# By-pair attention for block 0 alone, key and value loads on 128 partitions, three blocks that share half the features, and an order planned twice

## The chip, the cores and the metric

The kernel runs on one core of a Trainium2 chip. The metric is device time in microseconds (us) of one execution. Three runs of the kernel before stand at 640.6, 641.05 and 642.23 us; the median, 641.05 us, is what the change is compared with. Five engines work side by side: PE (TensorE, matmuls), DVE (VectorE), ACT (ScalarE), POOL (GpSimd) and SP, which here only issues transfers. Each takes its instructions strictly in the order in which the program lists them.

## The reference

Three stages, one after the other, on 2304 tokens of 512 features (4 batches of 576 tokens, 8 heads of 64):

```python
kv = einsum('bhsd,bhse->bhde', k, v)                 # one 64x64 matrix per batch and head
out = einsum('bhsd,bhde->bhse', q, kv)
x = out / sqrt(mean(out**2, -1) + 1e-6) * g_norm     # tokens x 512
h = x @ w_in                                         # 512 -> 2048
y = (h * tanh(softplus(h))) @ w_out                  # 2048 -> 512
h2 = y @ w2_in                                       # 512 -> 1024
z = h2 * softmax(h2)
out = layernorm(z) * g_ln @ w2_out                   # 1024 -> 512
```

The weights come as 8-byte floats. Every matmul of the two expert stages is done as three fp16 matmuls (high times high, high times low, low times high; `PASS`).

## The kernel before, in words

Tokens are cut into 6 blocks of 384 (`BLK`). The hidden features of the first expert stage are cut into 4 groups of 512; a *unit* (b, g) is one block with one group. `H` of a unit is 4 matmul groups of 12 (`h_mm`, L557), `Y` of a unit again 4 groups of 12 (`y_mm`, L597). The second stage works on 18 token tiles: `2` (`emit_H2`, L674) is 24 matmuls, `O` (`emit_O`, L757) is 24 matmuls, and between them stands a softmax and layer norm on DVE and ACT and a transposing DMA (`s_T`, tile lnT).

**Weights** arrive in 48 pieces of 512 KB (`PIECES`): first features 0 to 1023 of w_in (8 pieces) and of w_out (8), then the second halves, then the second stage's. Each piece is decoded from 8 bytes to a high and a low fp16 half: ACT L505, POOL L510, DVE L515 and L522, ACT L533 (high), DVE L540 or L542 (low). There are 5 staging buffers, so the load of a piece waits for an earlier piece's L522.

**Attention** has two forms. *By pair* (functions `e_*`) works on transposed tiles of two heads in fp32, all on PE: transposes of q (L288), kv (L246), q times kv (L304), the sums of squares as a matmul with ones (L317), and the spread of the result over partitions as another (L337). *By tile* (functions `a_*`) works on 128 tokens with fp16 halves: q is split on ACT and DVE, transposed by DMA (L386, tile qT), multiplied on PE (L398), squared, summed and scaled on ACT, DVE and POOL, split into halves, and transposed by DMA again (L446, tile xT). The result of either, xT of a block, is what `H` of that block reads. Before the change blocks 0 and 1 go by pair and blocks 2 to 5 by tile.

kv of a batch is made in four pairs of heads (`kv_pair`): the 576 tokens lie as 96 partitions x 6 rows, and each pair is 12 matmuls of 64 columns, each of two recorded passes.

**The order** is made by a planner (`Plan.order`): each task has an engine, a cost in us, tasks that it follows, and sometimes a due time. The planner walks through the time, and gives a free engine the ready task with the earliest due time. The due times are worked back from `nominal`, a table of times that the list `pe` of PE's units gives. The table walks units two blocks at a time over the first half of the features: H of (0,0), (0,1), (1,0), (1,1), then the second half of blocks 0 and 1, and from block 2 on all four groups of a block. Y of the halves is kept as a partial sum (`y_part`, `y_sum`) for blocks 0 and 1.

What the planner puts out is five fixed lists. All plain loads but that of q of block 0 stand on SP's list, those of the weights among them, as do the transposing DMAs.

Of the kernel before, what the change touches and what calls it, by code (L numbers as in the profile page):

```python
# [7 lines left out]
FP32 = mybir.dt.float32  # L8
# [24 lines left out]
class Plan:  # L33
    def __init__(self):
        self.tasks = {}

# [3 lines left out]

    def order(self):
        tasks = self.tasks
        index = {k: n for n, k in enumerate(tasks)}
        followers = {k: [] for k in tasks}
        for k, t in tasks.items():
            for a in t[3]:
                followers[a].append(k)

        seen, topo = set(), []

        def visit(k):
            stack = [(k, iter(tasks[k][3]))]
            seen.add(k)
            while stack:
                at, it = stack[-1]
                for a in it:
                    if a not in seen:
                        seen.add(a)
                        stack.append((a, iter(tasks[a][3])))
                        break  # L60
                else:
                    topo.append(at)
                    stack.pop()

        for k in tasks:
            if k not in seen:
                visit(k)
        due = {}
        for k in reversed(topo):
            d = 1e9 if tasks[k][5] is None else tasks[k][5]  # L70
            for f in followers[k]:
                d = min(d, due[f] - tasks[k][1] - tasks[k][4])
            due[k] = d
        waits = {k: len(t[3]) for k, t in tasks.items()}
# [8 lines left out]
        while True:  # L83
            best = None
            for e, ks in open_.items():
                if ks:
                    at = max(free[e], min(ready[k] for k in ks))
                    if best is None or at < best[0]:
                        best = (at, e)
            if best is None:  # L90
                break
            at, e = best
# [5 lines left out]
            for f in followers[k]:  # L98
                waits[f] -= 1
                ready[f] = max(ready[f], end + tasks[k][4])  # L100
                if not waits[f]:
                    open_[tasks[f][0]].append(f)
        assert len(out) == len(tasks), [k for k in tasks if waits[k] > 0][:20]
# [4 lines left out]
def tile_attn_moe_moe2(  # L108
# [19 lines left out]
    R = 3  # L128
# [6 lines left out]
    KP = 96  # L135
    KR = S // KP
    PASS = ((0, 0), (0, 1), (1, 0))
    NST, NDEC, NG, NM = 5, 5, 3, 3

# [45 lines left out]
    yorder = [(0, 0), (0, 1), (1, 0), (1, 1), (0, 2), (0, 3), (1, 2), (1, 3)]  # L185
    yorder += [(b, g) for b in range(2, NB) for g in range(4)]
    line = ["H", "H", "H", "Y", "H", "Y", "Y"]
    while line.count("H") < NU:
        line += ["H", "Y"]
    hs, ys = iter(units), iter(yorder)  # L190
# [11 lines left out]

    raw = {}

    def load_pair(b, i):
        t = yT[(0 if b == 1 else 2) + i].rearrange("p c a t -> p (c a t)").bitcast(FP32)[0:KP]
        raw[b, i] = t.rearrange("p (a h r d) -> p a h r d", a=2, h=2, r=KR)
        for a, src in enumerate((k, v)):
            nc.sync.dma_start(
                out=raw[b, i][:, a],  # L210
                in_=src[b, 2 * i:2 * i + 2].rearrange("h (p r) d -> p h r d", r=KR),
# [4 lines left out]
    def load_q(b):  # L216
# [3 lines left out]
        while done < BLK:  # L220
            bb, s = divmod(t0 + done, S)
            n = min(BLK - done, S - s)
            (nc.scalar if b == 0 else nc.sync).dma_start(
# [7 lines left out]

    kvp_t = {}
    kvf = {}

    def kv_pair(b, i):
# [18 lines left out]
    HALF = [slice(0, 64), slice(64, 128)]  # L254

    def kv_full(b, i):

        c = slice(i, i + 1) if b == 0 else slice(0, 4)
        nc.scalar.activation(
            out=kvf[b][HALF[0], c, HALF[0]], in_=kvp_t[b][HALF[0]], func=ACTF.Copy)  # L260
        nc.vector.tensor_copy(out=kvf[b][HALF[1], c, HALF[1]], in_=kvp_t[b][HALF[1]])

    def kv_zero():
        nc.gpsimd.memset(kvr[0], 0.0)

    def kv_hi(b):
        for o in HALF:
            nc.scalar.activation(
                out=kvr[b % 2][o, 0, :, o], in_=kvp_t[b][o], func=ACTF.Copy, scale=32.0)

    def kv_lo(b):
        p = kvp_t[b]
        for o in HALF:
            nc.vector.scalar_tensor_tensor(
                out=kvr[b % 2][o, 1, :, o], in0=p[o], scalar=32.0,
                in1=kvr[b % 2][o, 0, :, o], op0=ALU.mult, op1=ALU.subtract,
# [22 lines left out]
    def e_xo(b, c):  # L299
        qT = eq_t.pop((b, c)).rearrange("p (r t) -> p r t", r=R)  # L300
        p = ex_t[b, c] = psY.tile([128, BLK], FP32, tag=f"y{c % 3}", name="xoT")
        p = p.rearrange("p (r t) -> p r t", r=R)
        for lo, hi, bb in ((0, 128, 0),) if b == 0 else ((0, 64, 0), (64, 128, 1)):
            nc.tensor.matmul(  # L304
                out=p[:, :, lo:hi], lhsT=kvf[bb][:, c], rhs=qT[:, :, lo:hi], start=True, stop=True)
# [6 lines left out]
    def e_ms(b, c):  # L312
        p, tag = (psH, "h") if b == 0 else ((psA, "a"), (psY, "y3"))[c % 2]
        er_t[b, c] = p.tile([128, 512], FP32, tag=tag, name="rT")
# [75 lines left out]
    def a_xo(b, r):  # L390
        qT = qT_t.pop((b, r))
        p = psA.tile([128, H, D], FP32, tag="a", name="xo")
# [693 lines left out]
```

## Time and profile before

| what | value |
|---|---|
| median of 3 runs | 641.05 us |
| profiled execution, its own time | 646.7 us |
| span in its profile | 644.9 us |
| PE busy | 624.8 us (97%) |
| DVE busy | 307.7 us (48%) |
| ACT busy | 269.2 us (42%) |
| POOL busy | 93.1 us (14%) |
| read from memory | 39.33 MB |
| mean granted TensorE clock | 0.986 of full speed |

The span runs from the first to the last instruction. "Busy" of PE counts a matmul from its start to its modelled end, so it is not a share of peak. In the chain of waits each row is a piece of the work that ended last: start, length, what. A row of a group of instructions gives the count, the busy time and the mean of one, and the idle time of the engine just ahead of them with what ended it.

### The profile page before, as it was taken

What the parts mean: (1) busy time and instruction counts of PE and PEld (TensorE: products, weight loads), DVE (VectorE), ACT (ScalarE), POOL (GpSimd) and SP (SyncE); (2) the same over time, 40 slices, a digit from 0 to 9 for tenths busy, and PEclk for the clock granted to TensorE, in tenths of its full rate; (3) what the DMA queues carried; (4) which work ended last, traced back from release to release, by engine and by line L of the source; (5) the groups of instructions that cost most, each with busy time, mean ns of one, the idle gap of its engine ahead of it and who ended that gap; (6) DMA issues with size and microseconds to landing.
All of it is one profiled execution on the core that took longest, in us unless ns stands there. A gap on an engine that the chain in (4) does not pass through costs nothing.

```text
span 644.9 us, 9802 instructions
## 1 busy us (share of the span) xinstructions
PE 624.8 (97%) x4010; PEld 355.0 (55%) x4010; DVE 307.7 (48%) x529; ACT 269.2 (42%) x461; POOL 93.1 (14%) x125
## 2 busy tenths in 40 slices
PE   7899998999999999999999999999999999999995
PEld 5557564666666666666666656665444444444441
DVE  0667887921633144212321239952835555455540
ACT  2568756541523243422332247642523433433340
POOL 1516422100200022001200122500000000000000
PEclk9989798999999999999999999999999999999998
DMA  9985497365340025002200055500342232324322
GB/s 258 270 223 180 134 290 216 80 134 145 66 82 1 1 50 79 4 0 42 41 2 2 17 180 171 188 1 1 66 99 49 66 82 66 83 65 99 77 71 65
DMA packets 92605, 60.41 MB, mean 94 GB/s; under 512 B 65680, under 2 KB 86160, under 8 KB 92560
## 3 DMA queue, kind: packets, MB, share of 16 engines
q1 hardware_dynamic: 91360, 59.00, 36.6%
q10 hardware_dynamic: 1200, 0.79, 0.4%
q8 instruction: 31, 0.51, 0.3%
q14 instruction: 14, 0.11, 0.1%
HBM read 39.33 MB, written 4.72 MB: 68 GB/s over the span
## 4 chain that ended last, share of the span: by engine, by line
PE 89%; DMA 6%; DVE 2%; ACT 2%; issue 1%; POOL 1%; SPq 0%; DVEq 0%; ACTq 0%; POOLq 0%
PE hp L557 27%; PE y L597 26%; PE op L757 15%; PE h L674 14%; DMA st<-in_moe_w_in_dram 2%; PE kvp L246 2%; DMA st<-in_moe_w_out_dram 1%; PE qTp L288 1%; PE xo L398 1%; DMA yT<-in_v_dram 1%; DMA xT<-xhl 1%; PE xoT L304 1%; PE rT L337 1%; DMA lnT<-hl 1%; PE rT L317 1%
## 5 line engine op out<-in xcount | busy, mean ns | idle before, releaser
L597 PE MATMUL y<-g,w 128*128 128x384 f16 x1152 | 204.7, 330 | 2.5 <-ACT yT L610 2.5
L557 PE MATMUL hp<-xT,w 128*128 128x384 f16 x1152 | 201.3, 327 | 3.0 <-ACT w L533 1.9
L597 PEld LDWEIGHTS <-w 128*128 128x128 f16 x1152 | 112.6, 99 | 78.8 <-issue 6.5
L557 PEld LDWEIGHTS <-w 128*128 128x128 f16 x1152 | 111.7, 98 | 78.6 <-ACT w L533 2.2
L567 ACT ACTIVATE m<-hp 128x384 f32<-128x384 f32 x96 | 46.9, 488 | 132.5 <-PE hp L557 131.9
L757 PE MATMUL op<-w,lnT 128*128 128x512 f16 x432 | 97.7, 384 | 4.2 <-DMA lnT<-hl 4.2
L579 DVE SCALAR_TENSOR_TENSOR g<-m,g 128x768 f16<-128x768 f32 x48 | 46.7, 973 | 110.6 <-ACT g L574 110.5
L674 PE MATMUL h<-w,yT 128*128 128x512 f16 x432 | 96.2, 379 | 0.0
L757 PEld LDWEIGHTS <-lnT 128*128 128x128 f16 x432 | 42.6, 99 | 56.5 <-DMA lnT<-hl 4.7
L674 PEld LDWEIGHTS <-yT 128*128 128x128 f16 x432 | 42.3, 98 | 50.4
L510 POOL TENSOR_SCALAR st<-st 128x512 f32<-128x512 f32 x48 | 42.7, 895 | 91.7 <-ACT P L505 71.3
L515 DVE SCALAR_TENSOR_TENSOR st<-st 128x512 int32<-128x512 int32 x48 | 37.1, 787 | 16.8 <-POOL st L510 16.8
L574 ACT ACTIVATE g<-m 128x768 f16<-128x768 f32 x48 | 40.4, 841 | 1.8 <-PE y L597 0.8
L691 ACT ACTIVATE e<-h,nb 128x1024 f32<-128x1024 f32 x18 | 20.1, 1114 | 48.9 <-DVE nb L686 44.4
L505 ACT ACTIVATE P<-st 128x512 f32<-128x512 f32 x48 | 31.9, 673 | 14.2 <-DMA st<-in_moe_w_out_dram 7.8
L522 DVE SCALAR_TENSOR_TENSOR P<-P,st 128x512 int32<-128x512 int32 x48 | 35.6, 759 | 0.2
L418 POOL TENSOR_SCALAR ms<-ms 128x8 f32<-128x8 f32 x12 | 2.6, 216 | 228.2 <-DVE ms L413 228.2
L698 DVE SCALAR_TENSOR_TENSOR z<-h,e 128x1024 f32<-128x1024 f32 x18 | 22.0, 1225 | 21.4 <-ACT e L691 21.4
L724 POOL TENSOR_SCALAR var<-var 128x1 f32<-128x1 f32 x18 | 3.4, 190 | 192.6 <-DVE var L719 192.6
L738 ACT ACTIVATE hl<-z 128x1024 f16<-128x1024 f32 x18 | 19.0, 1056 | 28.9 <-DVE z L733 28.9
L705 ACT ACTIVATE e<-z,nmz 128x1024 f32<-128x1024 f32 x18 | 20.7, 1147 | 23.7 <-DVE nmz L701 23.7
L742 DVE TENSOR_TENSOR hl<-z,hl 128x1024 f16<-128x1024 f32 x18 | 22.0, 1224 | 15.7 <-ACT hl L738 15.7
(96 smaller groups left out, 421.6 us busy)
## 6 DMA issues: line engine op xcount, KB each, us to landing
st<-in_moe_w_in_dram SPq DMA_DIRECT2D x24, 512.0 KB, 6.7
st<-in_moe_w_out_dram SPq DMA_DIRECT2D x24, 512.0 KB, 4.3
yT<-in_k_dram SPq DMA_DIRECT2D x16, 288.0 KB, 7.9
yT<-in_v_dram SPq DMA_DIRECT2D x16, 288.0 KB, 8.1
out_dram<-osb SPq DMA_DIRECT2D x18, 256.0 KB, 2.0
qraw<-in_q_dram SPq DMA_DIRECT2D x3, 768.0 KB, 6.3
qraw<-in_q_dram SPq DMA_DIRECT2D x4, 384.0 KB, 8.6
qraw<-in_q_dram ACTq DMA_DIRECT2D x1, 768.0 KB, 6.9
```

Of the source, the lines that this page charges most:

```text
L505: nc.scalar.activation(out=P, in_=v[:, :, 1], func=ACTF.Copy, scale=2.0 ** -111)
L510: nc.gpsimd.tensor_scalar(out=v[:, :, 1], in0=v[:, :, 1], scalar1=0.0, scalar2=1.0, op0=ALU.mult, op1=ALU.mult)
L515: nc.vector.scalar_tensor_tensor(out=v[:, :, 0], in0=v[:, :, 0], scalar=29, in1=v[:, :, 1], op0=ALU.logical_shift_right, op1=ALU.bitwise_or)
L522: nc.vector.scalar_tensor_tensor(out=P.bitcast(I32), in0=P.bitcast(I32), scalar=3, in1=v[:, :, 0], op0=ALU.logical_shift_left, op1=ALU.bit ...
L557: nc.tensor.matmul(out=h_t[b, grp, i], lhsT=w1[:, c, wa, f:f + 128], rhs=xT_t[b][:, C * xa + c], start=(c == 0 and m == 0), stop=(c == C - ...
L567: nc.scalar.activation(out=m_t[b, grp, i // 2][:, i % 2], in_=h_t.pop((b, grp, i)), func=ACTF.Mish, scale=2.0 ** -16)
L574: nc.scalar.activation(out=g_t[b, grp][:, 0, 2 * i:2 * i + 2], in_=m_t[b, grp, i], func=ACTF.Copy, scale=64.0)
L579: nc.vector.scalar_tensor_tensor(out=g_t[b, grp][:, 1, j], in0=m_t.pop((b, grp, i)), scalar=64.0, in1=g_t[b, grp][:, 0, j], op0=ALU.mult, ...
L597: nc.tensor.matmul(out=y_t[cc][:, 0:BLK], lhsT=w2[:, grp * G + ii, wa, cc * 128:(cc + 1) * 128], rhs=g_t[b, grp][:, ga, ii], start=(first ...
L674: nc.tensor.matmul(out=hp[:, half], lhsT=y[:, c, ya, tok], rhs=w3[:, c, wa, half * 512:(half + 1) * 512], start=(m == 0), stop=(m == 3 * C ...
L698: nc.vector.scalar_tensor_tensor(out=z, in0=T[t, "hp"], scalar=2.0 ** -14, in1=T[t, "e"], op0=ALU.mult, op1=ALU.mult, accum_out=sz)
L757: nc.tensor.matmul(out=op, lhsT=lnT[:, K2 * la + kk], rhs=w4[:, kk, wa], start=(m == 0), stop=(m == 3 * K2 - 1),)
```

## The change

1. Only block 0 goes by pair. Block 1 goes by tile like the others, with its three products in PSUM banks y0 to y2, which Y uses later. kv of batch 0 is kept in fp32 (`kvf[0]`) and its fp16 halves are made from that copy.
2. k and v of two heads lie on 128 partitions (head, then 64 parts of 9 tokens), so a pair is 18 matmuls of 64 rows and 64 columns in place of 12 of 96 rows.
3. Blocks 0, 1 and 2 (`NI`) go through the first half of the features before any goes through the second; block 2 gets a partial sum too, and xT of block 2 lies in the buffer of yT of block 5.
4. The planner plans twice: the times of the first plan become the due times of the second. Some costs are changed, the first loads stand in a line written by hand, and q of block 0 is loaded from SP.

```diff
-    KP = 96
-    KR = S // KP
+    KR = 2 * S // 128
+    NI = 3
...
-    units = [(0, 0), (0, 1), (1, 0), (1, 1), (0, 2), (1, 2), (0, 3), (1, 3)]
-    units += [(b, g) for b in range(2, NB) for g in range(4)]
+    units = [(b, 2 * half + g) for half in range(2) for b in range(NI) for g in range(2)]
+    units += [(b, g) for b in range(NI, NB) for g in range(4)]
...
     for r in range(KR):
             for h in range(2):
                 nc.tensor.matmul(
                     out=p[64 * h:64 * h + 64, j],
-                    lhsT=t[:, 0, h, r],
-                    rhs=t[:, 1, h, r],
+                    lhsT=t[HALF[h], 0, r],
+                    rhs=t[HALF[h], 1, r],
...
-        p = psA.tile([128, H, D], FP32, tag="a", name="xo")
+        p, tag = (psY, f"y{r}") if b == 1 else (psA, "a")
+        p = p.tile([128, H, D], FP32, tag=tag, name="xo")
...
     def y_ends(b, grp):
-        first = grp == 0 or (b < 2 and grp == 2)
-        last = grp == 3 or (b < 2 and grp == 1)
+        first = grp == 0 or (b < NI and grp == 2)
+        last = grp == 3 or (b < NI and grp == 1)
...
-    LAND = 1.9
+    LAND, PAIR, QLD, PIECE = 2.0, 2.15, 3.0, 1.6
...
-    tiles = [(b, r) for b in range(2, NB) for r in range(R)]
+    tiles = [(b, r) for b in range(1, NB) for r in range(R)]
...
+    w, kv = (lambda f: ("ld", ("1", f))), (lambda b, i: ("ld", b, i))
+    plan.line([
+        ("ldq", 0), kv(0, 0), kv(0, 1), w(0), kv(0, 2), kv(0, 3), w(1), w(2), w(3),
+        ("ldq", 1), kv(1, 0), kv(1, 1), w(4), kv(1, 2), w(5), kv(1, 3), w(6), w(7),
+    ])
...
+    for at_time, key in plan.order():
+        if plan.tasks[key][5] is not None:
+            plan.tasks[key][5] = at_time
     order = plan.order()
```

Where the instructions stand now is shown at three places.

PE, from the first kv pair on, before (kvp is a pair's kv, qTp a transposed q, xoT q times kv, rT the sums and the spread):

```order
L246 MATMUL kvp<-yT_104 64x64 x12
L288 MATMUL qTp<-ident,qraw 64x128 x24
L246 MATMUL kvp<-yT_105 64x64 x12
L304 MATMUL xoT<-qT,kvr_91 128x384 x2
L317 MATMUL rT<-ones,sq 128x2 x3
L246 MATMUL kvp<-yT_106 64x64 x12
```

and in the change, up to the first matmul of H (hp):

```order
L269 MATMUL qTp<-ident,qraw 64x128 x18
L233 MATMUL kvp<-yT_104 64x64 x18
L269 MATMUL qTp<-ident,qraw 64x128 x6
L233 MATMUL kvp<-yT_105 64x64 x18
L283 MATMUL xoT<-qT,kvf 128x384 x2
L294 MATMUL rT<-ones,sq 128x2 x6
L233 MATMUL kvp<-yT_106 64x64 x18
L314 MATMUL rT<-ident,rho 64x128 x6
L283 MATMUL xoT<-qT,kvf 128x384
L233 MATMUL kvp<-yT_107 64x64 x18
```

Three q transposes now stand ahead of the first kv pair, and a pair has 18 matmuls where it had 12.

SP, from the loads of batch 1's last kv pairs on, before (st is a weight piece, yT the buffer that k and v lie in, qraw is q):

```order
L460 DMA st<-in_moe_w_in_dram 128x4x256 x2
L209 DMA yT_105<-in_k_dram 96x2x384
L209 DMA yT_105<-in_v_dram 96x2x384
L468 DMA st<-in_moe_w_out_dram 128x1024 x5
L223 DMA qraw<-in_q_dram 128x8x192
L468 DMA st<-in_moe_w_out_dram 128x1024 x3
L460 DMA st<-in_moe_w_in_dram 128x4x256 x5
```

and in the change:

```order
L195 DMA yT_105<-in_v_dram 128x576
L441 DMA st<-in_moe_w_in_dram 128x4x256
L363 DMA_TRANSPOSE qT<-qhl 128x8x128
L441 DMA st<-in_moe_w_in_dram 128x4x256
L363 DMA_TRANSPOSE qT<-qhl 128x8x128 x2
L449 DMA st<-in_moe_w_out_dram 128x1024 x2
L209 DMA qraw<-in_q_dram 128x8x192
L449 DMA st<-in_moe_w_out_dram 128x1024 x2
L427 DMA_TRANSPOSE xT<-xhl 128x8x128
L449 DMA st<-in_moe_w_out_dram 128x1024 x2
L427 DMA_TRANSPOSE xT<-xhl 128x8x128
L363 DMA_TRANSPOSE qT<-qhl 128x8x128
```

The transposes of blocks 1 and 2 now stand between the loads of the weights, where before no transpose came until all of w_out was loaded.

ACT at the end of the program, before (e is the softmax, hl the split of the layer norm, osb the copy of a finished `O`):

```order
L765 ACTIVATE osb<-op 128x512
L738 ACTIVATE hl<-z 128x1024
L691 ACTIVATE e,S__5745<-h_5674,nb 128x1024
L705 ACTIVATE e,sq<-z,nmz 128x1024
L738 ACTIVATE hl<-z 128x1024
L765 ACTIVATE osb<-op 128x512 x2
```

and in the change:

```order
L746 ACTIVATE osb<-op 128x512
L719 ACTIVATE hl<-z 128x1024
L672 ACTIVATE e,S__5738<-h_5660,nb 128x1024
L686 ACTIVATE e,sq<-z,nmz 128x1024
L746 ACTIVATE osb<-op 128x512 x6
```

Behind the last tile's softmax stand six copies of an `O` in place of two: on PE seven `O` of 24 matmuls follow the last `2`, where before three did.

## Rows read from the trace of the kernel before

**Rows 1.** The page, section 2: 40 slices of the span, busy tenths of DVE, granted PE clock

```profile
DVE  0667887921633144212321239952835555455540
PEclk9989798999999999999999999999999999999998
```

**Rows 2.** The chain of waits, 0 to 75 us: start, length, what (pieces left out)

```profile
0.72 0.40 SPq L209
...
63.45 1.87 POOL rho L329
...
66.91 3.95 PE y L597 x12
70.87 4.23 PE hp L557 x25
```

**Rows 3.** PE's matmuls of H, 27.5 to 70.8 us: count, busy us, mean ns, idle

```profile
L557 PE MATMUL hp<-xT,w 128*128 128x384 f16 x97 | 19.0, 337 | 2.9 <-ACT w L533 1.9 <-DVE w L542 1.0
```

**Rows 4.** The chain of waits, 95 to 125 us, round the only later stop of PE

```profile
96.78 8.62 DMA st<-in_moe_w_out_dram
...
108.66 3.76 PE y L597 x12
112.41 1.95 PE hp L557 x12
```

**Rows 5.** The chain of waits, 600 to 645 us

```profile
614.60 5.18 PE h L674 x24
619.78 10.23 PE op L757 x48
630.01 4.29 DMA lnT<-hl
...
634.35 7.00 PE op L757 x24
```

**Rows 6.** Groups of PE's instructions by pair for block 0, 5 to 27.5 us

```profile
L288 PE MATMUL qTp<-ident,qraw 128*64 128x128 f32 x48 | 4.9, 393 | 0.0
...
L337 PE MATMUL rT<-ident,rho 128*64 128x128 f32 x48 | 3.5, 279 | 0.2 <-POOL rho L329 0.2
L304 PE MATMUL xoT<-qT,kvr 128*128 128x384 f32 x8 | 3.3, 519 | 0.0
L317 PE MATMUL rT<-ones,sq 128*128 128x2 f32 x24 | 3.3, 254 | 0.0
```

**Rows 7.** Groups of PE's instructions, 70.8 to 437 us

```profile
L597 PE MATMUL y<-g,w 128*128 128x384 f16 x1069 | 188.6, 328 | 2.5 <-ACT yT L610 2.5
...
L398 PE MATMUL xo<-kvr,qT 128*128 128x128 f16 (+1 forms) x180 | 10.1, 220 | 0.0
L246 PE MATMUL kvp<-yT 96*64 96x64 f32 x192 | 7.3, 226 | 0.0
```

**Rows 8.** DVE's groups, 27.5 to 70.8 us: decode of a piece of w_in, low half of kv

```profile
L515 DVE SCALAR_TENSOR_TENSOR st<-st 128x512 int32<-128x512 int32 x11 | 8.0, 729 | 5.4 <-POOL st L510 5.4
L522 DVE SCALAR_TENSOR_TENSOR P<-P,st 128x512 int32<-128x512 int32 x11 | 7.9, 724 | 0.1
L542 DVE SCALAR_TENSOR_TENSOR w<-P,gs,w 128x512 f16<-128x512 f32 x8 | 5.9, 745 | 2.0 <-ACT w L533 2.0
...
L274 DVE SCALAR_TENSOR_TENSOR kvr<-kvp,kvr 64x256 f16<-64x256 f32 x2 | 0.8, 422 | 0.0
```

**Rows 9.** DVE's groups over the whole span: low half of g, a step of attention by tile

```profile
L579 DVE SCALAR_TENSOR_TENSOR g<-m,g 128x768 f16<-128x768 f32 x48 | 46.7, 973 | 110.6 <-ACT g L574 110.5
...
L439 DVE TENSOR_TENSOR xhl<-xf,xhl 128x512 f16<-128x512 f32 x12 | 8.3, 690 | 5.3 <-ACT xhl L434 5.3
```

**Rows 10.** ACT's group, 27.5 to 70.8 us: high half of kv

```profile
L268 ACT ACTIVATE kvr<-kvp 64x256 f16<-64x256 f32 x2 | 0.8, 378 | 0.5 <-DVE kvf L261 0.5
```

**Rows 11.** Transfers issued at 131 to 140 us: KB, median us from issue to landing

```profile
qraw<-in_q_dram SPq DMA_DIRECT2D x1, 768.0 KB, 5.1
```

**Rows 12.** Transfers of the whole span

```profile
xT<-xhl SPq DMA_TRANSPOSE x12, 3.1
```

More of the change, by code (lines that the diff above doesn't have):

```diff
@@ L39, in add, with line @@
         self.tasks[key] = [engine, cost, fn, [a for a in after if a is not None], lag, due]
+    def line(self, keys):
+        for a, b in zip(keys, keys[1:]):
+            self.behind.setdefault(b, []).append(a)
     def order(self):
@@ L43, in order @@
         index = {k: n for n, k in enumerate(tasks)}
+        edges = {k: [(a, tasks[a][4]) for a in t[3]] + [(a, 0.0) for a in self.behind.get(k, ())]
+                 for k, t in tasks.items()}
         followers = {k: [] for k in tasks}
[L45 to L67, printed above, removed]
+        for k, es in edges.items():
+            for a, lag in es:
+                followers[a].append((k, lag))
+        waits = {k: len(es) for k, es in edges.items()}
+        topo = [k for k in tasks if not waits[k]]
+        for k in topo:
+            for f, _ in followers[k]:
+                waits[f] -= 1
+                if not waits[f]:
+                    topo.append(f)
+        assert len(topo) == len(tasks), [k for k in tasks if waits[k] > 0][:20]
         due = {}
         for k in reversed(topo):
[L70 to L74, printed above, removed]
+            due[k] = 1e9 if tasks[k][5] is None else tasks[k][5]
+            for f, lag in followers[k]:
+                due[k] = min(due[k], due[f] - tasks[k][1] - lag)
+        waits = {k: len(es) for k, es in edges.items()}
         ready = {k: 0.0 for k in tasks}
@@ L299, in e_xo @@
     def e_xo(b, c):
-        qT = eq_t.pop((b, c)).rearrange("p (r t) -> p r t", r=R)
+        qT = eq_t.pop((b, c))
         p = ex_t[b, c] = psY.tile([128, BLK], FP32, tag=f"y{c % 3}", name="xoT")
[L302 to L305, printed above, removed]
+        nc.tensor.matmul(out=p, lhsT=kvf[0][:, c], rhs=qT, start=True, stop=True)
     def e_sq(b, c):
@@ L827, in tile_attn_moe_moe2 @@
             if b == 3:
-                free = [("kv", 2, i), ("put", ("2", 15))]
-            task(("ld", b, i), "S", 1.8, load_pair, (b, i), free, LAND)
-    ring("qhl", 3, ("xo", 1, 3))
+                free = [("kv", 3, i - 2) if i > 1 else ("kv", 2, i + 2), ("put", ("2", 15))]
+            task(("ld", b, i), "S", PAIR, load_pair, (b, i), free, LAND)
+    for b in range(B):
+        for i in range(4):
+            task(("kv", b, i), "P", 0.92, kv_pair, (b, i),
+                 [("ld", b, i), ("kv", b, i - 1) if i else None], 0.25)
@@ L881, in tile_attn_moe_moe2 @@
-    kv_after = {2: [("kvz",)], 3: [("xo", 2, r) for r in range(R)]}
-    order_a = [2] + [(2, r) for r in range(R)] + [3] + [u for u in tiles if u[0] > 2]
+    task(("ldq", 0), "S", QLD, load_q, (0,), (), LAND)
+    for c in range(4):
+        u = (0, c)
+        bank = f"y{c % 3}"
+        task(("qT", *u), "P", 0.95, e_qT, u,
+             [("ldq", 0), ("ident",)] + ring(bank, 1, ("qc", *u)), 0.25)
+        task(("qc", *u), "A", 0.49, e_qc, u, [("qT", *u)] + (
+            ring("qT", 3, ("xo", *u)) if c < 3 else ring("xhl", 2, ("xo", *u))))
@@ L890, in tile_attn_moe_moe2 @@
+    for b in range(B):
+        every = [("kvf", 0, i) for i in range(4)] + [("zero",)] if b == 0 else [
+            ("kv", b, i) for i in range(4)]
+        if b:
+            plan.tasks["kv", b, 0][3] += bank_a[b]
+        if b > 1:
+            every += [("xo", b - 1, r) for r in range(R)]
+        task(("kvh", b), "A", 0.75, kv_hi, (b,), every)
         task(("kvl", b), "V", 0.8, kv_lo, (b,), [("kvh", b)])
@@ L923, in tile_attn_moe_moe2 @@
             else:
-                x = [("xlo", b, c) for c in range(C)] if b < 2 else [
+                x = [("xlo", b, c) for c in range(C)] if b == 0 else [
                     ("xT", b, r) for r in range(R)]
@@ L943, in tile_attn_moe_moe2 @@
     last_of, prev_y = {}, None
-    for n, (b, grp) in enumerate(yorder):
+    for n, (b, grp) in enumerate(units):
         T0 = nominal["Y", b, grp]
@@ L983, in tile_attn_moe_moe2 @@
          [("glo", *u, i) for u in units for i in range(2)]
[L984 removed]
+         + [("ylo", b, c) for b in range(NI) for c in range(C)] + [("open",)], 0.0)
     for t in range(NT2):
```

170 lines of the change are left out of this document (63 added, 107 removed).

## The prediction

> **What bounds the kernel now.** I read the page first. PE is busy over nearly the whole span, DVE in its first sixth and hardly later, and the granted TensorE clock dips once, in the slices round 70 us [rows 1]. So the time is PE's work and the places where PE does not do it, and those are to be looked for early and at the very end. The chain of waits says where. Up to 70.87 us it jumps between engines: PE waits for POOL's rho at 63.45, and only at 70.87 does H of block 1 begin [rows 2]. By then 96 matmuls of H (the row counts the next group's first too) and one group of Y are done [rows 3, 2], that is 8 + 1 of the 192 groups of 12; a group takes 1.95 at the full clock [rows 4]. From there the chain is PE alone, with one stop: ACT's queue stands behind a weight piece that landed late, PE sits idle for 2.5 [rows 7], and its next group takes 3.76 [rows 4]. At the end PE waits 4.29 for the last transposed tile, and the last `O` takes 7.00 where one in the stream takes 5.18 [rows 5]. The groups of DVE show what the early phase consists of on that engine, the decode of the weights [rows 8]. So three things can be won: an earlier start of H of block 1, the stop at 106 us, the end.
>
> **The change, part by part.** I go against the profiled execution (646.7 us, span 644.9) and come to the median at the end.
>
> *Start, PE.* The order has q of block 0 first on SP, at 0.72 [rows 2]; q alone lands 5.1 after its issue [rows 11], so at 5.8. Until the last kv pair of batch 1 PE has, by the order of the change: block 0 by pair, 4.9 + 3.5 + 3.3 + 3.3 = 15.0 [rows 6]; 45 matmuls of H, 45 x 1.95/12 = 7.3; and 8 kv pairs. A pair of before is 24 passes; 8 pairs took 7.3 [rows 7], so a pass is 0.038 and a pair 0.92. The change has 36 passes a pair. No row shows 64-row operands. From below, 0.92 again, as if a pass that reads fewer rows cost that much less. From above, a pass that shares the array with nothing: the 8 passes of 384 columns took 3.3 [rows 6], 1.08 ns a column, so 64 columns cost 0.069 and a pair 2.5. I take the nearest row, the kv passes themselves: 36 x 0.038 = 1.38. That makes 8 x 1.38 = 11.0, in sum 33.3, and PE is never short of loads there as I see it: 5.8 + 33.3 = 39.1. Then come the two high halves on ACT and the two low ones on DVE, 2 x 0.38 + 2 x 0.42 = 1.6 [rows 10, 8], with handovers 1.9: 41.0.
>
> *Start, DVE.* From there DVE is the engine that is waited for. Up to the low half of the first piece of w_out its list has 20 instructions: 4 of L515 (0.729), 3 of L522 (0.724), 4 low halves (0.745), one low half of g (0.97), 8 steps of block 1's attention (0.69) [rows 8, 9]: 14.6, so 55.6. Nine more (2, 2, 2 and 3 of these kinds, 6.5) end with the low half of the third piece, 62.0. PE has by then done two groups of Y, slow ones perhaps, since it waited for them. Now the order has one q-times-kv tile of block 2 (10.1 for 12 tiles, 0.84 each [rows 7]), the third group of Y, and H of block 1: 62.0 + 0.84 + 1.95 = 64.8. xT of block 1 covers itself: its last low half is the third of those nine, 57.7, and it lands 3.1 later [rows 12], 4 us before it is read. Those 4 us are all the cover; SP issues weight loads between its transposes, and a transpose that stands behind a waiting one comes late.
> So H of block 1 begins at 64.8 with 8 + 3 groups done, against 70.87 with 8 + 1: 6.1 + 2 x 1.95 = **10.0 won**. Block 1's work by pair on PE goes with it, and is not counted twice.
>
> *Tiles and pairs later.* Before, 12 tiles stand behind that point; in the change 15 in all, 4 of them ahead: one less, **0.8 won**. The 8 pairs of batches 2 and 3 stand in the stream where PE is never idle: 8 x 0.46 = **3.7 lost**.
>
> *The stop at 106 us.* Two blocks on half the features are 8 units, 8 x 4 x 1.95 = 62 of PE; three are 12, 94. The second half's pieces are due 31 later, and DVE, at 9 tenths until 130 [rows 1], gets its time: 2.5 + 3.76 - 1.95 = **4.3 won** [rows 7, 4]. What is late next is xT of block 2. Its last tile on PE is followed by five groups of Y, 9.75, and then by H that reads it. The way there is five steps on ACT and DVE of 0.7 [rows 9], POOL's 1.9 [rows 2] and 3.1 of landing [rows 12], 8.5 without handovers or queues: I put **1.5 lost**, between 0 and 4.3, a stop as the old one.
> The partial sum of block 2 adds four copies on ACT and four sums on DVE, at nothing, since DVE is at 1 to 4 tenths then [rows 1]; without that cover some 2.
>
> *The end.* Behind the last `2` stand seven `O`, so 6 x 5.18 = 31 of PE work lies ahead of the last one; the wait for its tile began 10.23 after the last `2` and took 4.29 [rows 5], so 14.5 are needed. 4.29 + 7.00 - 5.18 = **6.1 won**. A transposed tile waits for the buffer of the `O` five before, which ends 10.4 after the last `2`, and still lands in time.
>
> Sum: 10.0 + 0.8 - 3.7 + 4.3 - 1.5 + 6.1 = 16.0. The profiled execution would take 630.7. The median stands 5.65 under the profiled one, so **625 us**.
>
> **The rivals.**
> - *The pairs are cheaper and DVE is less crowded.* For it: heads now differ in rows and in columns; against: no row shows it. At 0.92 a pair the start wins 8 x 0.46 = 3.7, the stream another 3.7, and without the new stop 1.5: 616. With a start of DVE that has less to wait for, 613.
> - *The pairs are dear.* Both heads of a pair write the same PSUM bank. At 2.5 a pair, 1.1 over my price, 16 pairs lose 17.9, more than all I count: 643, no change. For it: only that the passes of before, which share rows, cannot tell. Against: the q transposes too write both halves of one bank in turn, and cost 4.9 / 48 = 0.10 for 128 columns [rows 6], under the price of an unshared pass. By the Trainium skill, "TensorEngine Tiling (Array Packing)", section "Restrictions and Gotchas", different row tiles cannot access the same PSUM bank simultaneously; by this rule the two heads would not run side by side, and this rival would be the result. The same page's "Tiling Modes" says that tiles operate independently; no row of before tells which holds here.
> - *SP's list stalls the start, and it is slower than before.* The transposes of blocks 1 and 2 wait for DVE at the head of SP's list, with weight pieces behind them; ACT's list then stands at the piece that has not landed, with the copies that free PE's banks behind it. That is the stop at 106 us, 4.3 each time. It decides from the fourth such stop on, or if H of block 1 begins after 81. For it: the list now has 12 transposes among the weights of the first stage, before none. Against: pieces are due late, and DVE, not the loads, sets the pace. At six stops: 645.
> - *The start is no earlier.* PE and DVE are both full there, so any lost overlap counts; then only the end and the old stop are won, less the pairs and the new stop, and two or three slow groups: 639 or more, at the edge of no change.
>
> **How the numbers follow.** My forecast, 617 to 634, has 0.66; the cheap pairs 0.17; the dear pairs 0.05; the stalls of SP's list 0.07; no earlier start 0.05. About 0.3% (1.9 us) is what a measurement here can tell from no change. Faster by more than that: the first two and a little of the last, 0.84; within: 0.09; slower: the stalls, 0.07. The range holds the forecast and reaches to the cheap pairs below and to the edge of the dear ones above, 613 to 637. Its width comes from a pair (0.92 to 2.5), the start (59 to 71) and the new stops (0 to 4.3).
>
> **What would show it.** In the profile of the change: H of block 1 begins near 65 us, with three groups of Y ahead; a kv pair takes near 1.4; DVE has no idle time to speak of from 41 to 62; there is no DMA wait in the chain after 70; the end shows six `O` in a row and no wait for lnT. The prediction is wrong if a pair takes 0.9 or over 2, if the chain shows PE behind xT of block 1 or behind a weight piece more than once, or if H of block 1 begins later than 71.

## The result, and the profile after

The changed kernel takes 633.16 us (median of 4 runs, 632.47 to 633.54); the kernel before, run beside it, 641.64 (4 runs, 640.6 to 644.08). The ratio is 0.9861, 95% interval 0.9831 to 0.9892: 8.5 us less. The predicted 625 is 8 too low; the range and the sign hold. The profiled execution of the change took 633.54, span 631.8, mean granted clock 0.994.

The page of the changed kernel, section 2 (40 slices; busy tenths of PE and DVE, granted PE clock), against [rows 1]:

```profile
PE   8896988999999999999999999999999999999997
DVE  1789998931113261224321359927777245555400
PEclk9997999999999999999999999999999999999999
```

DVE is at 8 tenths or more from the third slice to the eighth, where before it first came to 8 in the fifth, and the deepest dip of the clock stands one slice earlier. The timeline of PE after the change (start, length, operation, count, in brackets the idle time ahead of it and what ended it):

```profile
41.74 0.87 PE L376 MATMUL xo<-kvr,qT 128*64 128x128 f16 x24
...
54.14 0.82 PE L578 MATMUL y<-g,w 128*128 128x384 f16 x2 [2.69 <-ACT w L514]
56.52 5.65 PE L578 MATMUL y<-g,w 128*128 128x384 f16 x22 [1.56 <-DVE w L521]
62.01 0.83 PE L376 MATMUL xo<-kvr,qT 128*128 128x128 f16 x12
62.68 2.11 PE L578 MATMUL y<-g,w 128*128 128x384 f16 x12
64.98 5.21 PE L538 MATMUL hp<-xT,w 128*128 128x384 f16 x31 [0.18 <-DMA xT<-xhl]
...
93.57 4.06 PE L578 MATMUL y<-g,w 128*128 128x384 f16 x24 [1.73 <-ACT yT L591]
99.34 11.86 PE L538 MATMUL hp<-yT,w 128*128 128x384 f16 x72 [1.70 <-DMA yT<-xhl]
```

H of block 1 begins at 64.98 with eight groups of H and three of Y done (36 passes stand in these rows), where before it began at 70.87 with eight and one [rows 2, 3]. PE no longer stops at 106 us [rows 4], but it stops at 93.57 and at 99.34. The first of these is the stop of before, come forward and shorter: in both kernels Y waits for ACT's four copies of the partial sum of block 0 (L610 before, L591 now), which stand in ACT's list behind a weight piece. The chain of waits of before, and then ACT's timeline after the change:

```profile
105.48 0.68 ACT P L505
...
108.23 0.38 ACT yT L610
```

```profile
90.09 0.69 ACT L486 ACTIVATE P<-st 128x512 f32<-128x512 f32 x1 [2.40 <-DMA st<-in_moe_w_in_dram]
...
93.05 1.62 ACT L591 ACTIVATE yT<-y 128x384 f32<-128x384 f32 x4
```

The second is new. It is xT of block 2 (it lies in a buffer of yT), as the chain of waits of the changed kernel tells:

```profile
27.91 1.26 PE kvp L233 x36
...
34.48 1.20 PE kvp L233 x36
...
73.85 5.39 DMA st<-in_moe_w_in_dram
...
89.10 1.98 POOL rho L398
...
93.68 5.52 DMA yT<-xhl
```

The transpose takes 5.52 from its issue, where 3.1 was the median of the twelve before [rows 12]. A kv pair of 36 passes takes 1.20, 33 ns a pass. The group of its later pairs, in the groups of PE from 70 to 437 us, answers to [rows 7]; the chain's end answers to [rows 5]:

```profile
L233 PE MATMUL kvp<-yT 64*64 64x64 f32 x288 | 10.1, 221 | 0.0
```

```profile
591.30 36.27 PE op L738 x168
```

Eight pairs cost 10.1 where they cost 7.3. At the end seven `O` run without a gap, 36.27 or 5.18 each; nothing waits for lnT.

The sum of the profiles: start 5.9 + 2 x 1.95 = 9.8 won; one tile less 0.8 won; pairs 2.8 lost; the stop behind ACT's copies 4.3 before and 1.7 now, 2.6 won; stops for xT of block 2, 1.7, and of block 3 at 240 us, 0.7, together 2.4 lost; the end 6.1 won; and behind the last `O` it is 4.2 to the end of the span, before 3.55 [rows 5], 0.7 lost. That is 13.4, and the spans differ by 13.1. The medians differ by 8.5 only.

### The profile page after: what moved, and what is told of

Read it like the earlier page. It is cut to its first block, busy times and chain, and to the rows that moved or that the text cites. A ratio compares the mean times of both kernels' runs of the same rounds, so it can differ in the third digit from the quotient of the medians.

```text
span 631.8 us, 10070 instructions
## 1 busy us (share of the span) xinstructions
PE 613.8 (97%) x4136; PEld 347.5 (55%) x4136; DVE 310.4 (49%) x534; ACT 269.7 (43%) x459; POOL 96.3 (15%) x126
## 4 chain that ended last, share of the span: by engine, by line
PE 84%; DMA 6%; DVE 3%; ACT 2%; POOL 2%; SPq 1%; issue 1%; POOLq 0%; ACTq 0%
PE hp L538 26%; PE y L578 25%; PE op L738 15%; PE h L655 15%; PE kvp L233 2%; DMA yT<-in_v_dram 2%; POOL rho L398 1%; DMA qraw<-in_q_dram 1%; PE xo L376 1%; DMA yT<-xhl 1%; DMA st<-in_moe_w_in_dram 1%; DMA xT<-xhl 1%; DMA st<-in_moe_w_out_dram 1%; ACT P L486 1%; POOL st L491 1%
## 5 line engine op out<-in xcount | busy, mean ns | idle before, releaser
L578 PE MATMUL y<-g,w 128*128 128x384 f16 x1152 | 202.3, 329 | 6.0 <-ACT w L514 2.7
L538 PE MATMUL hp<-xT,w 128*128 128x384 f16 x960 | 165.4, 326 | 2.0 <-DMA xT<-xhl 0.9
L738 PE MATMUL op<-w,lnT 128*128 128x512 f16 x432 | 95.2, 379 | 0.0
L491 POOL TENSOR_SCALAR st<-st 128x512 f32<-128x512 f32 x48 | 43.1, 904 | 99.9 <-ACT P L486 95.2
L555 ACT ACTIVATE g<-m 128x768 f16<-128x768 f32 x48 | 40.3, 840 | 12.6 <-PE y L578 11.9
L496 DVE SCALAR_TENSOR_TENSOR st<-st 128x512 int32<-128x512 int32 x48 | 36.7, 780 | 10.9 <-POOL st L491 10.9
L396 POOL TENSOR_SCALAR ms<-ms 128x8 f32<-128x8 f32 x15 | 5.1, 342 | 222.6 <-DVE ms L391 222.1
L503 DVE SCALAR_TENSOR_TENSOR P<-P,st 128x512 int32<-128x512 int32 x48 | 36.2, 769 | 0.2
L538 PE MATMUL hp<-yT,w 128*128 128x384 f16 x192 | 33.0, 326 | 1.7 <-DMA yT<-xhl 1.7
L666 DVE TENSOR_REDUCE mx<-h 128x1 f32<-128x1024 f32 x18 | 22.0, 1223 | 20.6 <-PE h L655 20.6
```

What stands on the lines that cost most here:

```text
L491: nc.gpsimd.tensor_scalar(out=v[:, :, 1], in0=v[:, :, 1], scalar1=0.0, scalar2=1.0, op0=ALU.mult, op1=ALU.mult)
L496: nc.vector.scalar_tensor_tensor(out=v[:, :, 0], in0=v[:, :, 0], scalar=29, in1=v[:, :, 1], op0=ALU.logical_shift_right, op1=ALU.bitwise_or)
L503: nc.vector.scalar_tensor_tensor(out=P.bitcast(I32), in0=P.bitcast(I32), scalar=3, in1=v[:, :, 0], op0=ALU.logical_shift_left, op1=ALU.bit ...
L538: nc.tensor.matmul(out=h_t[b, grp, i], lhsT=w1[:, c, wa, f:f + 128], rhs=xT_t[b][:, C * xa + c], start=(c == 0 and m == 0), stop=(c == C - ...
L555: nc.scalar.activation(out=g_t[b, grp][:, 0, 2 * i:2 * i + 2], in_=m_t[b, grp, i], func=ACTF.Copy, scale=64.0)
L578: nc.tensor.matmul(out=y_t[cc][:, 0:BLK], lhsT=w2[:, grp * G + ii, wa, cc * 128:(cc + 1) * 128], rhs=g_t[b, grp][:, ga, ii], start=(first ...
```

## The experiments

All medians, each with the ratio to the kernel before in runs on the same chip and its 95% interval. The median of the kernel before lies between 641.64 and 644.39 in these series, so between kernels of different series the ratios are the better measure:

| kernel | us | ratio |
|---|---|---|
| before, once more (x1) | 642.96 | 1.0004 (0.9974 to 1.0034) |
| before, planned twice (x9) | 645.45 | 1.0046 (1.0022 to 1.007) |
| change with 96 partitions and two blocks (x10) | 634.96 | 0.9877 (0.9834 to 0.992) |
| change with 96 partitions (x3) | 635.79 | 0.9879 (0.984 to 0.9917) |
| change with two blocks (x4) | 631.21 | 0.9803 (0.9765 to 0.9841) |
| the change | 633.16 | 0.9861 (0.9831 to 0.9892) |
| change planned once (x2) | 636.62 | 0.9901 (0.9863 to 0.9939) |
| change, head by head (x5) | 645.74 | 1.0044 (1.0017 to 1.0072) |
| change, rho planned at 2.5 (x6) | 632.27 | 0.9836 (0.9797 to 0.9875) |
| change, dummy passes (x7) | 632.97 | 0.9842 (0.9807 to 0.9877) |
| two blocks, dummy passes (x8) | 630.95 | 0.9805 (0.977 to 0.984) |
| two blocks, part of the decode on POOL (x11) | 633.42 | 0.9861 (0.9826 to 0.9896) |
| two blocks, durations of its own trace (x12) | 632.11 | 0.9802 (0.9761 to 0.9842) |

### Was the profiled execution of before an odd one?

What was expected:

> The kernel before, unchanged, profiled and timed once more. Theory: its profiled execution of 646.7 us was an odd one, 2.7 us above the longest of its four timed runs; a second one lies within 1.5 us of 641.6, its H of block 1 begins near 68 instead of 70.87 us or the stop at 106 us is shorter, and so the 5.65 us that the prediction took off as an offset of every profile were none. Rival: every profile of this kernel lies some 5 us above the median, 645 to 648 us again, and the changed kernel's (0.4 us above) is the odd one.

Ten runs of the unchanged kernel lie between 640.21 and 646.29, 17 of its copy beside them between 640.0 and 647.17. The time goes with the mean granted clock of the run: over these runs and those beside the other experiments the median is 641.0 at 0.992 (15 runs), 642.8 at 0.989 (35) and 646.8 at 0.986 (8); the profiled run here, at 0.984, took 645.82. So 646.7 at 0.986 was one of the long runs and no offset of a profile; the theory is wrong in that the second profile is a long one too, 2.9 above its median. The changed kernel's four runs have 0.994 or 0.995 and lie within 1.1 us. In the second profile of before H of block 1 begins at 69.62 and the stop at 107 us is 2.24, both a little better than in [rows 2, 7]. The fourteen profiled executions here lie between 1.1 under the median of their kernel and 5.65 above it, so a forecast can't carry that distance from one kernel to another.

### One part at a time

The second planning by itself, on the kernel before (x9):

```diff
+    for at_time, key in plan.order():
+        if plan.tasks[key][5] is not None:
+            plan.tasks[key][5] = at_time
     order = plan.order()
```

What was expected:

> The kernel before with its order planned a second time from the times of the first planning, and nothing else (a tile of block 1 is taken at its first use, not by a chunk's number). H of block 1 then stands behind two groups of Y instead of one, H of block 2 behind 384 passes of Y instead of 360. Theory (the second planning alone is worth what its absence cost the changed kernel, some 3 us): 639.5 us, 0.995 of the kernel before. Rival: without the attention of block 1 out of the way the second planning has nothing to work with, 642 us, 0.998 or more.

It makes the kernel slower, 645.45 beside 641.76. The timeline of PE of this kernel:

```profile
70.50 4.71 PE L557 MATMUL hp<-xT,w 128*128 128x384 f16 x28
...
107.81 3.67 PE L597 MATMUL y<-g,w 128*128 128x384 f16 x12 [3.99 <-ACT yT L610]
```

H of block 1 begins at 70.50 with one group of Y more ahead, which is 2.3 won, and the old stop grows from 2.5 [rows 7] to 3.99. Neither theory foresaw that. The profiles (645.85 here, 646.7 before) show no loss, the medians do; what is lost in the usual run was not found.

On the changed kernel the same lines do the contrary; x2 takes them out.

What was expected:

> The changed kernel with its order planned once, not twice. In this order H of block 1 stands behind 8 groups of H and 2 of Y instead of 8 and 3, H of block 2 behind 96 passes of Y instead of 120, and H of block 3 behind 504 instead of 540. Theory (the second planning fills the stretch in which TensorE would wait): one group of Y later at 2.0 us, and a longer stop before H of block 2, whose tiles come no earlier: 1.7 us more than the 1.7 now; 635 to 638 us, H of block 1 still at 65 us or a little before it. Rival (the stretch is bound by the decoding on VectorE and the order on TensorE only shifts the stops): 633 us, within 0.3% of the changed kernel.

636.62, 3.5 us above the change by the medians and 2.6 by the ratios: the theory holds in size. In its trace PE stands still for 4.9 us behind ACT's high halves of weights, in place of 3.3, and 3.7 behind xT of block 2, in place of 1.7.

Two blocks that share half the features, on 128 partitions (x4: `NI = 2`), and on 96 partitions (x10, x3):

```diff
-    KR = 2 * S // 128
+    KP = 96
+    KR = S // KP
...
-                    lhsT=t[HALF[h], 0, r],
-                    rhs=t[HALF[h], 1, r],
+                    lhsT=t[:, 0, h, r],
+                    rhs=t[:, 1, h, r],
```

What was expected:

> The changed kernel with two blocks that share half the features instead of three, the rest as it is, order planned twice. Theory: H of block 1 then stands behind two groups of Y (2.0 us lost at the start), a stop like that of 4.3 us at 106 us comes back, since the eight groups of H of block 2 no longer stand there, and the stop of 1.7 us at 99 us before H of block 2 goes: 636 to 639 us. Rival: the third block brings nothing, since its own tiles are late by as much as the stop that it fills: 632 to 634 us.

What was expected:

> The changed kernel with k and v on 96 partitions and two blocks that share half the features: beside the kernel before with its order planned twice it differs in the attention of block 1 (by tile, not by pair), in the planner's durations and in the features' order. Theory: that is the part that brings the most; the two blocks bring 2 us as in the changed kernel, the 96 partitions cost 1 to 2: 633 us, 0.984 of the kernel before, and 6 us less than the kernel before planned twice. Rival: it brings little by itself, the parts win only together: 637 us or more, 0.991.

What was expected:

> The changed kernel with k and v on 96 partitions again, 12 passes a head and pair instead of 18; the order on every engine is the same but for these passes. Theory: two pairs take 0.85 us again instead of 1.20, which gives 2.7 us back over the eight pairs behind H of block 1, and the start pays for it: loads at 270 GB/s instead of 295 to 340, the first pair of the second batch lands 1 to 2.5 us after 27.8 us and H of block 1 moves by as much; in sum within 2 us of the changed kernel, 631.5 to 635. Rival (the wider pieces are what starts H of block 1 early): H of block 1 at 68 us or later, 636 to 638 us.

*By tile.* x10 is 10.5 below x9 (0.9877 against 1.0046). This step, the attention of block 1 by tile with the planner's durations, the first loads' line, q of block 0 on SP and the order of features that come with it, is as large as the whole gain of the change. Little of it is the earlier start: behind two groups of Y in both, H of block 1 begins at 69.44 in x10 and 70.50 in x9. In the traces the end brings 6.0 (no wait for lnT) and the stop near 106 us 5.2 (3.99 and a slow group in x9, 0.47 in x10). Which of the things that changed together brings the end, no run tells. The timeline of PE of x10, the end of its chain of waits, and that of x9:

```profile
69.44 5.85 PE L539 MATMUL hp<-xT,w 128*128 128x384 f16 x35
...
105.18 2.11 PE L579 MATMUL y<-g,w 128*128 128x384 f16 x12 [0.47 <-ACT yT L592]
```

```profile
593.55 36.27 PE op L739 x168
```

```profile
629.32 4.30 DMA lnT<-hl
...
633.66 6.83 PE op L757 x24
```

*Third block.* The theory fell, and its rival did not go far enough: two blocks are faster, not slower. The timeline of PE of x4:

```profile
55.35 0.82 PE L538 MATMUL hp<-xT,w 128*128 128x384 f16 x2 [5.18 <-ACT w L514]
58.31 3.38 PE L538 MATMUL hp<-xT,w 128*128 128x384 f16 x10 [2.14 <-DVE w L523]
...
66.45 3.74 PE L538 MATMUL hp<-xT,w 128*128 128x384 f16 x22
...
102.21 2.11 PE L578 MATMUL y<-g,w 128*128 128x384 f16 x12 [0.50 <-ACT yT L591]
```

H of block 1 is later here, at 66.45 with two groups of Y instead of three, 3.4 us of PE's work behind the change. This profiled execution, 634.36, is the longest of its seven; in x8, also two blocks, H of block 1 begins at 64.03, 1.0 behind:

```profile
64.03 6.18 PE L538 MATMUL hp<-xT,w 128*128 128x384 f16 x37
```

But the stop near 106 is 0.5, not the 4.3 expected, and no other stop of PE behind H of block 1 is longer than 0.4. The cleanest pair is x7 and x8, both with dummy passes (12 and 20, at different places), in the same series: three blocks 632.54 to 634.07 (5 runs), two blocks 630.45 to 631.58 (6 runs). The third block costs 2.0 us. On 96 partitions nothing of it can be told (635.79 and 634.96).

*Partitions.* x3 stands 2.6 above the change, x10 3.7 above x4; by the ratios it is 1.2 and 4.8, so the size is known only roughly. The price of the passes comes back as expected, the later pairs being shorter, but the start pays more than I allowed; the rival is nearer. The timeline of PE of x3:

```profile
30.05 1.55 PE L234 MATMUL kvp<-yT 96*64 96x64 f32 x24 [1.80 <-DMA yT<-in_v_dram]
31.53 5.90 PE L539 MATMUL hp<-xT,w 128*128 128x384 f16 x21
...
68.36 6.84 PE L539 MATMUL hp<-xT,w 128*128 128x384 f16 x41
```

The first pair of batch 1 starts at 30.05 instead of 27.91, PE stands still for 1.80 and the 21 passes of H that come soon after take 281 ns each, where 163 is the price at the full clock (the granted clock is 0.66 from 28 to 38 us in this execution). H of block 1 begins at 68.36, 3.4 after the change's.

### Why a kv pass is cheap

```diff
-        for r in range(KR):
-            for h in range(2):
+        for h in range(2):
+            for r in range(KR):
```

What was expected:

> The changed kernel with the two loops over a pair of k and v swapped: all 18 passes of one head (rows 0 to 63, lower half of the bank) before the 18 of the other, where they alternate now. Theory: a pass costs its 33 ns in either order, two pairs 1.2 us, and the time stays (633 us, within 0.3%). Rival: 33 ns holds only because two heads work side by side in different rows of the array; head by head two pairs take some 2.4 us, the eight pairs behind H of block 1 cost 4.8 us more, 637 to 639 us.

The rival wins, and by more than it asked for: 645.74, 12.6 above the change and no longer faster than before. The timeline of PE:

```profile
35.68 2.13 PE L233 MATMUL kvp<-yT 64*64 64x64 f32 x36
37.74 0.66 PE L538 MATMUL hp<-xT,w 128*128 128x384 f16 x3
...
69.99 5.20 PE L538 MATMUL hp<-xT,w 128*128 128x384 f16 x31
```

A pair takes 2.06 (from 35.68 to 37.74) instead of 1.20, 57 ns a pass instead of 33. The eight pairs behind H of block 1 lose 8 x 0.86 = 6.9, and H of block 1 begins 5.0 later: 11.9 of the 12.6. So the price that I took for a pass holds only in the order in which the two heads alternate. Different rows are not needed for it: in x3 the two heads lie on the same 96 rows and alternate between the halves of the columns, and 24 passes take 0.85, 35 ns each. Whether alternating passes run side by side in the array, or passes of one head wait for the sum that the pass ahead of them writes, no run tells apart.

### Does the new stop, or the clock, cost anything?

```diff
-        task(("rho", *u), "G", 2.0, a_rho, u, [("ms", *u)] + ring("rho", 3, ("xf", *u)))
+        task(("rho", *u), "G", 2.5, a_rho, u, [("ms", *u)] + ring("rho", 3, ("xf", *u)))
```

What was expected:

> The changed kernel with one number of the planner changed: rho on GpSimd is planned at 2.5 us instead of 2.0 (its two steps take 0.5 and 1.9 us in the changed kernel's trace). H of block 2 then stands behind 144 passes of Y instead of 120. Theory: the stop of 1.7 us at 99 us before H of block 2 goes and the one at 93 us stays or shrinks: 2 us less, 631 us, or 0.983 of the kernel before. Rival: the stretch to 110 us is bound by the decoding on VectorE, which is 90% busy there, and the stop only moves: 633 us, 0.986 of the kernel before.

632.27 lies between the two. The profiled execution was the longest of its six, 637.0. In its timeline of PE the stop before H of block 2 is gone and another has come:

```profile
58.18 1.45 PE L376 MATMUL xo<-kvr,qT 128*128 128x128 f16 x12 [4.04 <-DMA qT<-qhl]
...
98.03 9.64 PE L578 MATMUL y<-g,w 128*128 128x384 f16 x48 [2.49 <-ACT yT L591]
```

It is inconclusive as to 1 us. In this one long execution the stop moves, as the rival has it; for the usual run that is not shown. Then the dummy passes, in the change (x7) and with two blocks (x8, 20 in front of `("H", 0, 1, 3)`):

```diff
+        if key == ("Y", 0, 0, 0):
+            keep_warm(12)
         fn()
```

What was expected:

> The changed kernel with 12 dummy passes of 512 columns on TensorE in front of the first passes of Y, where it now waits 2.7 us for a piece of the weights; their result is read by nobody. Theory: the granted clock of 0.74 between 52 and 65 us, at which 22 passes of Y take 257 ns each, follows from TensorE standing still at 51.4 to 56.5 us; with the gap filled the 22 passes take about 175 ns, 1.8 us less, and the mean clock rises from 0.994 to 0.997: 631.3 us, 0.983 of the kernel before. Rival: the clock falls there for another reason (the loads and the other engines at work, or chance), and nothing is won: 633 us or up to 1 us more.

What was expected:

> The kernel with two blocks that share half the features and 20 dummy passes in front of the last group of H of block 0, where TensorE waits 5.2 us for the weights. Theory: the clock of 0.61 between 52 and 65 us rises, the 24 passes behind the wait take 167 to 176 ns instead of 221 to 338, 2.3 us less; 629 us, 0.977 of the kernel before, the fastest of all. Rival: the weights come when they come, the passes behind the wait are hidden by the next wait for weights, 631 us, 0.980 as without the dummy passes.

The timeline of PE of x7, and its stretches of 52 to 65 and 80 to 110 us (sum of the stretch, then busy time of PE, its weight loads, DVE, ACT, POOL with counts, granted clock, DMA share, GB/s):

```profile
40.37 0.87 PE L376 MATMUL xo<-kvr,qT 128*64 128x128 f16 x24
...
49.92 2.75 PE L991 MATMUL idle<-kvr 128*128 128x512 f16 x12
...
55.16 2.12 PE L578 MATMUL y<-g,w 128*128 128x384 f16 x12 [1.87 <-DVE w L521]
...
63.20 7.00 PE L538 MATMUL hp<-xT,w 128*128 128x384 f16 x42
...
92.83 5.48 PE L578 MATMUL y<-g,w 128*128 128x384 f16 x24 [2.63 <-ACT yT L591]
99.18 11.86 PE L538 MATMUL hp<-yT,w 128*128 128x384 f16 x72 [0.87 <-DMA yT<-xhl]
```

```profile
52.00:65.00 13.00, 9.62 (x63) 5.05 (x61) 12.70 (x18) 7.34 (x13) 5.92 (x8) 1.00 1.03 241
...
80.00:110.00 30.00, 26.50 (x161) 15.49 (x160) 25.33 (x36) 21.15 (x38) 14.10 (x14) 0.94 0.72 201
```

The first of these stretches in the changed kernel, and then the second in x8:

```profile
52.00:65.00 13.00, 9.11 (x49) 4.68 (x50) 12.67 (x19) 8.71 (x16) 6.11 (x7) 0.74 0.99 219
```

```profile
80.00:110.00 30.00, 29.28 (x181) 17.54 (x180) 28.65 (x39) 21.21 (x39) 11.86 (x11) 1.00 0.79 242
```

Half of the theory holds: with the gap filled the granted clock is 1.00 instead of 0.74, a pass of Y takes 177 ns (12 in 2.12) instead of 257. H of block 1 begins at 63.20 instead of 64.98, but 1.4 of these 1.8 are not the dummy passes': this execution is ahead by as much already at 40.37, where block 1's first product stands at 41.74 in the changed kernel's trace. And the rest is worth nothing: PE stops for 2.63 at 92.83 instead of 1.73 at 93.57, the clock falls there instead (0.94 from 80 to 110 us), H of block 2 begins at 99.18 instead of 99.34, and the time is 632.97. What PE wins it waits away: between 37.9 and 99.2 us the chain of waits of x7 has no piece of PE, but DVE, ACT, POOL and transfers, and DVE is busy for 12.7 of the 13 us from 52 to 65. In x8 it is the same: 630.95, the time of x4. From 80 to 110 us its PE is busy for 29.3 us where x7's is for 26.5: there the stops of 2.63 and 0.87 are missing; the one for ACT's copies is 0.72.

### Can DVE be relieved?

```diff
-            nc.vector.tensor_tensor(out=lo, in0=P, in1=hi, op=ALU.subtract)
+            eng = nc.gpsimd if on_pool(u) else nc.vector
+            eng.tensor_tensor(out=lo, in0=P, in1=hi, op=ALU.subtract)
```

What was expected:

> The kernel with two blocks that share half the features, and the low part of every second piece of the second weights formed on GpSimd instead of VectorE (eight subtractions of 128 x 512; no row shows one there, it is planned at 1.3 us). Theory: up to 100 us the decoding on VectorE sets the time (29.6 of the 30 us from 80 to 110 us busy), so 8 x 0.7 = 5.6 us less of it bring the passes forward; H of block 1 stands behind three groups of Y and the total falls by 2 to 5 us: 626 to 629 us, 0.973 to 0.978 of the kernel before. Rival: the subtraction is slow on GpSimd or slows VectorE beside it, or a transfer is the next bound, and the time stays at 631 us, 0.980, or rises.

The rival: 633.42, 2.2 slower than two blocks without it by the medians and 3.7 by the ratios. The groups of x11, 50 to 105 us (count, busy us, mean ns):

```profile
L503 DVE SCALAR_TENSOR_TENSOR P<-P,st 128x512 int32<-128x512 int32 x19 | 18.1, 973 | 0.0
L496 DVE SCALAR_TENSOR_TENSOR st<-st 128x512 int32<-128x512 int32 x20 | 17.3, 891 | 0.0
...
L525 POOL TENSOR_TENSOR w<-P,w 128x512 f16<-128x512 f32 x5 | 7.3, 1467 | 2.0 <-ACT w L514 2.0
```

The subtraction takes 1.47 on POOL, and DVE's own steps beside it take 973 and 891 ns, where in x4 the same lines take 898 and 765 in the same stretch. What was taken off DVE's list came back in the length of what stayed on it: H of block 1 begins at 66.00 behind three groups of Y, in x8 at 64.03 behind two, which is even. The loss is PE's stop for ACT's copies, 0.50 in x4 and 0.72 in x8:

```profile
101.80 2.11 PE L582 MATMUL y<-g,w 128*128 128x384 f16 x12 [2.48 <-ACT yT L595]
```

The last run plans two blocks with the durations of its own trace (five lines of the planner).

What was expected:

> The kernel with two blocks that share half the features, planned (twice) with the durations that its own trace shows from 50 to 105 us, where VectorE and GpSimd work side by side: the steps of the decoding at 0.77, 0.90 and 0.73 or 0.88 us on VectorE instead of 0.72 and 0.77, 0.87 instead of 0.7 on GpSimd, rho 2.4 instead of 2.0. The order on TensorE changes in a few places only, none ahead of the wait of 5.2 us for weights. Theory: durations that are nearer to the trace no longer change what bounds the stretch, the work of VectorE; 630 to 632 us, 0.979 to 0.983 of the kernel before. Rival: the plan that knows them puts the decoding of the first weights ahead of other work, the wait of 5.2 us shrinks by 2 or more: 628 to 629 us, 0.977.

The theory: the ratio, 0.9802, is inside what was expected, and 632.11 a tenth above its 632. The 5.2 us of waiting for high halves are 2.0 and 2.2 at two places here, and the time stays.

## Why the prediction was right, and where it was wrong

- **Start: right.** 10.0 won were predicted, with H of block 1 at 64.8 behind 8 + 3 groups; it is 64.98, and 9.8 (8.5 against the second profile of before, with its 69.62). The chain that I followed, DVE's list from the kv halves on, is the one that sets it: the low half of w_out's first piece ends at 56.5 where I put 55.6, that of the third at 62.8 where I put 62.0, and a faster PE gains some 0.4 (x7). What I did not see is that PE's passes of Y ran at a lower clock behind the wait; it cost hardly anything, for the same reason.
- **Pairs: mis-sized.** 1.38 was put for a pair, 1.20 to 1.26 is measured, so 2.8 lost and not 3.7. The reason given ("a pass is 0.038") was right by luck of the order: head by head a pass is 57 ns (x5). The two bounds, 0.92 and 2.5, held both. The rival of the dear pairs did not come: both halves of one bank are written in turn at 33 ns a pass. The rule of the Trainium skill that I set beside it ("TensorEngine Tiling (Array Packing)", "Restrictions and Gotchas": different row tiles cannot access the same PSUM bank simultaneously) does not show here as a price: the order that changes row tile at each pass is the faster one, 1.20 against 2.06. Whether two passes are ever in the bank at the same time, no run shows.
- **The stop at 106 us, "4.3 won": mis-sized, wrong cause.** It is not gone but stands at 93.57 with 1.7, so 2.6 are won. It is not "three are 12" units that shorten it: with two blocks it is 0.5 (x4, x10). The step that shortens it is the part that x10 has and x9 has not.
- **"1.5 lost, between 0 and 4.3": nearly the right size.** xT of block 2 costs 1.7, though the way there was longer than I had it: its rho took 1.98 on POOL and its landing 5.52 instead of 3.1. A stop of 0.7 for xT of block 3 was not in the sum. With what is left of the old stop, the stops cost 4.1 where I counted 1.5. The third block brings no gain for them: 2.0 us faster without it (x8 against x7).
- **The end: right.** 6.1 won, seven `O` in a row. The 0.7 behind the last `O` I had not counted.
- **"The median stands 5.65 under the profiled one": the step that failed most.** The sum was 16.0 and the profiles differ by 13.2, 2.8 off; then I took 5.65 off the result, and that was no property of profiles but of one long run of before at a lower mean clock (x1: 640 to 647 in the same kernel). The changed kernel's profile lies 0.4 above its median. Without that step I would have said 630.7; the median is 633.16. And the part of the gain in the profiles that only undid the long run is not in the medians: 13.1 against 8.5. Which of the terms are smaller in a usual run of before no trace shows, since both its profiled executions were long ones. That the time is inside the range is due to the width of the range (613 to 637), not to this step.
- **The signs, and two readings.** DVE was busy for 19.6 of the 21 us from 41 to 62, as said. But DMA waits came in the chain after 70, a weight piece at 73.85 (5.39) and xT of block 2 at 93.68 (5.52): the rival of SP's list was there in kind, not in size (its own "645 at six stops" would by its sums be 651). Rows 1 show three dips of the clock, not one, and DVE at 6 to 9 tenths until 130 us and at 9 again in two slices later.

The change as a whole is three gains and a loss. The step from x9 to x10, the attention by tile with what goes with it, brings most, and most of that at the end and at the old stop. The 128 partitions bring some 3 us (x3, x10; 1.2 to 4.8). The second planning, harmful on the kernel before, brings some 3 in the changed one (x2). The third block takes 2 us back. Without it the kernel takes 631.21, or 630.95 with the dummy passes, the fastest measured here.

## What to carry to other kernels

Compare a forecast's sum with the median only after asking how far runs of the same kernel lie apart: one profiled execution can be a long one, and the distance to its median does not go over to the next kernel. In a stretch where the chain of waits runs through other engines, filling PE's gaps moved the stops and left the sum (x7, x8); look at the chain, and at the list of the engine that is full, first. That a shorter list there would win, no run here shows: the one that took work off DVE (x11) lost. And where a matmul uses a part of the array only, price it in the order in which the parts follow each other.

## What the runs showed of the hardware

The order of passes on 64 x 64 parts of the array changes their price from 33 to 57 ns (x5). TensorE's clock stood at one of two levels, 1.2 or 2.4 GHz, so the granted clock of a stretch is a mean of 0.5 and 1. It fell in stretches with a standstill: 0.74 from 52 to 65 us, with waits of 2.69 and 1.56, and in x4 0.61, with 5.18 and 2.14. It stayed at 1.00 there when the first wait was filled with passes that nobody reads (x7). The stop of 1.73 at 93.57 did not bring it down (1.00 from 80 to 110 us), the one of 2.63 in x7 did (0.94).

DVE and POOL slow each other. The timeline of x4, both engines:

```profile
71.19 1.21 POOL L491 TENSOR_SCALAR st<-st 128x512 f32<-128x512 f32 x1 [1.08 <-ACT P L486]
71.77 1.16 DVE L503 SCALAR_TENSOR_TENSOR P<-P,st 128x512 int32<-128x512 int32 x1
...
74.32 0.68 DVE L503 SCALAR_TENSOR_TENSOR P<-P,st 128x512 int32<-128x512 int32 x1
```

The same step takes 1.16 beside POOL and 0.68 without it. Over the whole trace of x4, of the 96 such steps of the decode (L496, L503) none of the 52 without a POOL step beside them takes over 0.9; of the other 44, 22 take 1.1 or more. POOL's own step (L491) takes 0.65 where no DVE step runs beside it (6 of 48), and 0.87 in the median beside one. The Trainium skill says so much ("Perfetto Trace Analysis", "Optimizing Scalar/DVE Operations"): the two share an SBUF read port, so that moving work between them might not help. The trace agrees: x11 lost 2.2 us.
